# Sums of squares read one slot later, and scale products with one operand in PSUM, in a fused attention, SwiGLU and top-1 MoE kernel

## The chip, the core and the metric

The kernel runs on one core of a Trainium2 chip. The metric is device time in microseconds (us) of one execution. A measurement of this kernel is the median of several runs.

The core's engines run side by side, each through its own queue of instructions in order: TensorE (PE, with its weight loads shown as PEld), VectorE (DVE), ScalarE (ACT), GpSimd (POOL) and SyncE (SP), which here only issues DMAs. SBUF is the core's large memory, PSUM the small one into which TensorE writes.

## The reference

Three stages in a row; what one gives is the next one's input.

```python
# 1: attention with decay, B, H, S, D = 4, 8, 576, 64
scores = (q @ k^T) / sqrt(D)
cum = cumsum(log(clip(f, 0.0001, 1.0)))            # along the sequence
scores = where(causal, -1e9, scores + cum[:, :, :, None] - cum[:, :, None, :])
attn = softmax(scores);  x = (attn @ v)            # -> 2304 tokens x 512
# 2: SwiGLU, 512 -> 1536 -> 512
g = x @ w_gate;  y = (g * sigmoid(g) * (x @ w_val)) @ w_out
# 3: top-1 of 8 experts, 512 -> 1024 -> 512
e = argmax(y @ r_gate);  out = softmax prob of e * (relu(y @ w1[e]) @ w2[e])
```

## The kernel before, in words

Products are made from two 16-bit (or rounded 32-bit) halves of each operand. So that an operand fits 16 bits, it is first multiplied by a power of two that follows from its sum of squares. Such a scale is made in two steps. ACT squares the data and adds each partition's squares up (`accum_out`, into a tile `am` for q and k, `sq` for v, `totw` for the weights). Then `pow2_scale` asks TensorE for a tiny product with a matrix of eights (`onesf`), which leaves the total in each partition of a PSUM tile `tot`; three integer operations of DVE on one or two numbers turn it into a power of two, and a copy takes its inverse out. `tot` comes from the same ring of three PSUM banks (`ps_s`, tag `s`) as the score tiles `ps`.

The attention works on 16 pairs of heads (4 batches with 4 pairs). A pair has 4 items, and `slot(i)` records for item i: `part1(i)` (scores on TensorE, running maximum on DVE at L311, exponentials on ACT at L321), `part2(i - 1)` (16-bit halves of the probabilities: DVE's cast at L343, POOL's differences at L346 and L357, then a transposing DMA `pt<-p` at L360), `pv(i - 2)` (attention times v on TensorE, L381, and the normalised `xn`), and a piece of the next pair's preparation. For pair P + 1 that is `scales` with the first slot of pair P, `prep_v` with the second, `prep` for one head with the third and for the other with the fourth. `scales` holds the two squares (L189, their result `jk` is thrown away), `pow2_scale`, three tiny products `c` on DVE (L197) and a small ACT operation `nc` (L202). `prep` makes the halves `qks` of q and k on ACT (L224, L229) and DVE (L228) and issues the transposing DMA `qkt<-qks` (L231), without which the pair's scores can't begin (L256).

Beside the attention the SwiGLU weights are decoded and split, as a list of tasks: `w_dec` (a load, ACT, DVE, POOL, then squares on ACT at L866) for two halves of `w_gate`, `w_split` of it (`pow2_scale`, then ACT at L880 and DVE at L881), the same for `w_val`, and so on for six blocks. `unit(u)` is one block of SwiGLU on TensorE: `g` and `v` (L491), then `yp` (L544). Units run beside the later attention slots and go on alone after them; then come the experts (L1177, L1220).

What is recorded here is not the order in which the engines run it. The kernel is built with a scheduler (`schedule_with_timeline_sim=True`) that plays the program through with times of its own and writes each engine's queue from that. Semaphores and ring buffers follow that order.

Of the kernel before, what the change touches and what calls it, by code (L numbers as in the profile page):

```python
# [7 lines left out]
F32 = mybir.dt.float32  # L8
# [3 lines left out]
I32 = mybir.dt.int32  # L12
# [3 lines left out]
ALU = mybir.AluOpType  # L16
# [11 lines left out]
def kernel(  # L28
# [145 lines left out]
    def load_qk(P, a):  # L174
        if P < NPAIR:
            load_heads(qk_in[(2 * P + a) % NQK], (q, k)[a], P // NP, 2 * (P % NP))
# [5 lines left out]

    stt = {}

    def scales(P):
        am = st_p.tile([128, 2], F32, tag="am", bufs=2, name="am")
        jk = qks_p.tile([128, 3 * NCH, 2, D], F16, tag="qks", name="jk").rearrange("p (a c) h d -> p a c h d", a=3)
        for a in range(2):
            act.activation(  # L189
                out=jk[:, a].rearrange("p c h d -> p h c d"), in_=qk_in[(2 * P + a) % NQK], func=ACTF.Square,  # L190
                accum_out=am[:, a:a + 1],
            )
        sc = st_p.tile([128, 2, 2], F32, tag="sc", name="sc")
        pow2_scale(sc[:, 0, :], sc[:, 1, :], [am])
        c = st_p.tile([128, 3], F32, tag="c", name="c")
        for i, (w, f_) in enumerate(((1, 0.125), (0, 8.0), (1, -0.125))):
            vec.scalar_tensor_tensor(  # L197
                out=c[:, i:i + 1], in0=sc[:, w, 0:1], scalar=f_, in1=sc[:, w, 1:2], op0=ALU.mult, op1=ALU.mult
            )
        nc_ = st_p.tile([128, 2, 128], BF16, tag="nc", bufs=2, name="nc")  # L200
        h0 = P // NP * H + 2 * (P % NP)
        act.activation(  # L202
            out=nc_, in_=pick[:, h0:h0 + 2].rearrange("p (h o) -> p h o", o=1).to_broadcast([128, 2, 128]),
            func=ACTF.Copy, scale=c[:, 1:2],
        )
        stt[P] = (sc, (c, nc_))
# [29 lines left out]
    def prep_v(P):  # L236
        i = P % NV
        sb_ = sv[:, 0, P // NP:P // NP + 1]
        vs = vs_p.tile([128, 2, NCH, 2, D], F16, tag="vs", name="vs")
        for hh in range(2):  # L240
            src = v_in[i][:, hh]
            act.activation(out=vs[:, hh, :, 0, :], in_=src, func=ACTF.Copy, scale=sb_)
            vec.scalar_tensor_tensor(
                out=vs[:, hh, :, 1, :], in0=src, scalar=sb_, in1=vs[:, hh, :, 0, :], op0=ALU.mult, op1=ALU.subtract
            )
        vsp[P] = vs
# [193 lines left out]
    def slot(i):  # L440
        P = i // 4
        r = i % 4
        if i < NI:
            part1(i)
        if 0 <= i - 1 < NI:
            part2(i - 1)
        if 0 <= i - 2 < NI:
            pv(i - 2)
        if i % (4 * NP) == 10 and P // NP + 1 < B:
            v_scale(P // NP + 1)  # L450
        if P + 1 < NPAIR:
            if r == 0:
                scales(P + 1)
            if r == 1:
                prep_v(P + 1)
                if P + 2 < NPAIR:
                    load_v(P + 2)
            if r == 2:
                prep(P + 1, 0)
            if r == 3:  # L460
                prep(P + 1, 1)
                load_qk(P + 2, 1)
                load_qk(P + 3, 0)
# [305 lines left out]
        act.dma_start(out=y_d[NT:NT + 1, :], in_=zr)  # L769
        act.dma_start(out=g_d[NT:NT + 1, :], in_=zr[:, 0:1])  # L770

    def pow2_scale(dst, inv, parts):
        n = dst.shape[1]
        tot = ps_s.tile([128, 512], F32, tag="s", name="tot")[:, 0:n]
        for i, x in enumerate(parts):
            pe.matmul(
                out=tot, lhsT=onesf, rhs=x, start=(i == 0), stop=(i == len(parts) - 1), skip_group_check=True
            )
        ti = tot.bitcast(I32)
        vec.tensor_scalar(  # L780
            out=ti, in0=ti, scalar1=24, scalar2=23, op0=ALU.logical_shift_right, op1=ALU.logical_shift_left
        )
        vec.tensor_scalar(
            out=ti, in0=ti, scalar1=float(49 * EXP1), scalar2=float(48 * EXP1), op0=ALU.max, op1=ALU.add
        )
        vec.tensor_scalar(
            out=dst.bitcast(I32), in0=ti, scalar1=-1.0, scalar2=float(254 * EXP1), op0=ALU.mult, op1=ALU.add
        )
        vec.tensor_copy(out=inv, in_=tot)

    VB = H * S * D // 128
    vflat = v.rearrange("b h s d -> b (h s d)").rearrange("b (p n) -> b p n", p=128)
# [2 lines left out]
    def v_scale(b):  # L795
        sq = st_p.tile([128, 4], F32, tag="sq", bufs=1, name="sq")
        n = VB // 4
        for i in range(4):
            t = s_p.tile([128, 576], F32, tag="s", name="vr")[:, 0:n]
            sp.dma_start(out=t, in_=vflat[b, :, i * n:(i + 1) * n])  # L800
            act.activation(out=t, in_=t, func=ACTF.Square, accum_out=sq[:, i:i + 1])
        pow2_scale(sv[:, 0, b:b + 1], sv[:, 1, b:b + 1], [sq[:, i:i + 1] for i in range(4)])

    def unscale(b, j0, j1):
        rv = sv[:, 1, b:b + 1]
# [55 lines left out]
    def w_dec(j, i, h):  # L861
        f0 = 256 * j + 128 * h
        if h == 0:
            tops[j, i] = st_p.tile([128, 2], F32, tag="totw", name="totw")
        t = dec[j, i, h] = decode((w_gate, w_val)[i].rearrange("(k p) f -> p k f", p=128)[:, :, f0:f0 + 128], KD)
        act.activation(  # L866
            out=(wg16, wv16)[i][:, j, :, 0, 128 * h:128 * h + 128], in_=t, func=ACTF.Square,
            accum_out=tops[j, i][:, h:h + 1],
        )

    def w_split(j, i):
        tot = tops.pop((j, i))
        w16 = (wg16, wv16)[i]
        s1 = sw[:, 0, i, j:j + 1]
        pow2_scale(s1, sw[:, 1, i, j:j + 1], [tot[:, h:h + 1] for h in range(2)])
        for h in range(2):
            f0 = 128 * h
            src = dec.pop((j, i, h))
            hi, lo = w16[:, j, :, 0, f0:f0 + 128], w16[:, j, :, 1, f0:f0 + 128]
            act.activation(out=hi, in_=src, func=ACTF.Copy, scale=s1)  # L880
            vec.scalar_tensor_tensor(out=lo, in0=src, scalar=s1, in1=hi, op0=ALU.mult, op1=ALU.subtract)  # L881
# [11 lines left out]
    NJ = KF // 2  # L893
    tasks, mark, markw = [], {}, {}
    for j in range(NJ):
        for i in range(2):
            tasks += [lambda j=j, i=i, h=h: w_dec(j, i, h) for h in range(2)]
            tasks.append(lambda j=j, i=i: w_split(j, i))
        tasks.append(lambda j=j: unscale(0, j, j + 1))
        mark[j] = len(tasks)  # L900
        tasks += [lambda fk=fk: wo_dec(fk) for fk in (2 * j, 2 * j + 1)]
        markw[j] = len(tasks)
        if j >= NJ - 3:
            tasks.append(lambda j=j: free.__setitem__(0, [0, 1, 2] if j == NJ - 3 else [0]))
    done = [0]

    def upto(n):
        while done[0] < min(n, len(tasks)):
            tasks[done[0]]()
            done[0] += 1  # L910
# [195 lines left out]
    PRE0, PRE = 2, 43  # L1106
    start()
    upto(PRE0)
    scales(0)
    v_scale(0)  # L1110
    prep(0, 0)
    prep(0, 1)
    load_qk(1, 1)
    load_qk(2, 0)
    prep_v(0)
    load_v(1)
    first = 4 * NP + 2
# [321 lines left out]
```

## Time and profile before

| | |
|---|---|
| median of 3 runs | 1042.72 us (1039.12 to 1043.49) |
| the profiled execution's own time | 1036.55 us |
| its span, first to last instruction | 1034.8 us |
| busy share of the span | PE 86%, DVE 61%, ACT 54%, POOL 38% |
| mean granted TensorE clock | 0.933 |

The profiled execution is one run; its span lies 1.75 us below its own time and its time 6.2 us below the median of the three runs. Busy shares are means over stages that differ: the first 205 us hold the first attention slots and all the weight decoding, the stretch from 205 to 590 us the attention and SwiGLU together, and the rest SwiGLU alone, the routing and the experts.

### The profile page before, as it was taken

To read this page: it belongs to the slowest core of one execution; us is meant where nothing else is said; L and a number is where in the kernel's file an instruction comes from. 1 tells how busy PE (TensorE), PEld (TensorE's weight loads), DVE (VectorE), ACT (ScalarE), POOL (GpSimd) and SP (SyncE) were. 2 spreads that over 40 slices of the span, in tenths; PEclk is the share of its full clock that TensorE was granted. 3 is DMA by queue.
4 is the path that set the end of the run, shared out by engine and by line. 5 is a ranking of instruction groups with operands and counts; after the bars stand their busy time and mean duration, and the time that the engine had idled before them with its cause. 6 is when DMAs were issued, how large, how long until landed. Compare 5 with 4: busy or idle time off the path is not lost.

```text
span 1034.8 us, 19815 instructions
## 1 busy us (share of the span) xinstructions
PE 885.4 (86%) x7003; PEld 738.0 (71%) x7029; DVE 632.2 (61%) x1829; ACT 558.0 (54%) x1208; POOL 397.6 (38%) x473
## 2 busy tenths in 40 slices
PE   1545557989889988899899999999789899999995
PEld 0333436867667776788688878888668799899894
DVE  6999879497577575567765443234326787656440
ACT  5987988476576565556554231213225455555441
POOL 1567767364255234344444222222225643111101
PEclk9995557999999998999999999999898899999998
DMA  8897997258776768566754440203329987754430
GB/s 241 201 225 209 227 193 167 85 131 156 139 154 142 168 113 161 115 110 150 105 109 108 113 123 2 41 2 83 51 35 219 273 239 214 207 170 152 149 104 33
DMA packets 314409, 145.30 MB, mean 140 GB/s; under 512 B 279649, under 2 KB 292065, under 8 KB 314308
## 3 DMA queue, kind: packets, MB, share of 16 engines
q1 hardware_dynamic: 310016, 133.63, 55.7%
q0 software_dynamic: 4096, 10.24, 3.9%
q8 instruction: 56, 0.92, 0.4%
q14 instruction: 45, 0.37, 0.2%
q10 hardware_dynamic: 196, 0.14, 0.1%
HBM read 81.62 MB, written 10.31 MB: 89 GB/s over the span
## 4 chain that ended last, share of the span: by engine, by line
PE 42%; DMA 7%; issue 6%; ACT 3%; DVE 2%; POOL 2%; SPq 1%; POOLq 0%; DVEq 0%; ACTq 0%
PE bank L1220 9%; PE bank L1177 8%; PE yp L544 8%; PE v L491 7%; PE g L491 6%; DMA pair<-yt 1%; DMA out_dram<-o,ix 1%; POOL xg L1051 1%; PE px L381 1%; DMA qkt<-qks 1%; DMA pt<-p 1%; DMA pair<-words 1%; ACT st L321 1%; DMA wr<-in_moe_w_dram 1%; DVE st L311 1%
## 5 line engine op out<-in xcount | busy, mean ns | idle before, releaser
L491 PE MATMUL v<-xr,wv 128*128 128x256 f16 x1296 | 162.4, 281 | 0.0
L491 PE MATMUL g<-xr,wg 128*128 128x256 f16 x1296 | 161.4, 278 | 0.5 <-DMA xr<-xs 0.5
L491 PEld LDWEIGHTS <-wg 128*128 128x128 f16 x1296 | 123.6, 100 | 26.8 <-issue 9.2
L491 PEld LDWEIGHTS <-wv 128*128 128x128 f16 x1296 | 128.9, 101 | 18.9 <-issue 1.0
L346 POOL TENSOR_TENSOR p<-st,p 128x128 f16<-128x128 f32 (+3 forms) x128 | 108.7, 854 | 79.1 <-issue 52.4
L531 POOL TENSOR_TENSOR lo<-t,hi 128x512 fp32r<-128x512 f32 x54 | 71.5, 1324 | 148.6 <-ACT hi L530 123.4
L321 ACT ACTIVATE st<-st,nb,c 128x64 f32<-128x64 f32 (+4 forms) x160 | 102.6, 643 | 1.2
L381 PE MATMUL px<-vs,pt 128*128 128x64 f16 x1280 | 58.7, 203 | 41.0 <-DMA pt<-p 30.0
L343 DVE CAST p<-st 128x64 f16<-128x64 f32 (+4 forms) x160 | 71.8, 464 | 30.7 <-ACT st L321 21.9
L381 PEld LDWEIGHTS <-pt 128*128 128x128 f16 x1280 | 52.4, 106 | 52.4 <-DMA pt<-p 35.1
L514 ACT ACTIVATE t<-g,gscale 128x512 f32<-128x512 f32 (+3 forms) x72 | 39.3, 571 | 75.5 <-PE g L491 75.5
L256 PE MATMUL ps<-qkt 128*128 128x64 f16 (+2 forms) x192 | 56.7, 311 | 25.9 <-DMA qkt<-qks 11.3
L357 POOL TENSOR_TENSOR p<-st,p 128x64 f16<-128x64 f32 (+1 forms) x128 | 54.2, 425 | 61.5 <-DVE p L343 30.6
L1220 PE MATMUL bank<-whi,h 128*128 128x512 f32 x200 | 66.9, 400 | 4.8 <-ACT h L1182 4.8
L983 POOL DMA_INDIRECT out_dram<-o,ix x24 | 26.6, 1110 | 113.8 <-ACT o L1222 71.2
L311 DVE CUSTOM_DVE_ANT_0 st<-ps,zero 128x64 f32<-128x64 f32 (+3 forms) x160 | 55.6, 376 | 24.2 <-PE ps L264 21.0
L517 DVE SCALAR_TENSOR_TENSOR t<-t,g 128x512 f32<-128x512 f32 x54 | 36.9, 684 | 54.3 <-ACT t L514 54.2
L530 ACT ACTIVATE hi<-t 128x512 fp32r<-128x512 f32 x54 | 33.8, 625 | 60.8 <-DVE t L524 60.8
L949 DVE TENSOR_TENSOR wlo<-wr,whi 128x1024 fp32r<-128x1024 f32 x48 | 57.7, 1245 | 14.1 <-ACT whi L948 12.3
L257 PE MATMUL ps<-qkt 128*128 128x64 f16 (+2 forms) x192 | 59.9, 315 | 0.0
L544 PE MATMUL yp<-wohi,hi 128*128 128x512 f32 x144 | 59.7, 414 | 0.0
L1177 PE MATMUL bank<-xh,whi 128*128 128x320 f32 (+1 forms) x192 | 58.9, 309 | 0.5 <-ACT xh L93 0.5
(300 smaller groups left out, 2274.2 us busy)
## 6 DMA issues: line engine op xcount, KB each, us to landing
wr<-in_moe_w_dram SPq DMA_DIRECT2D x72, 512.0 KB
vr<-in_v_dram SPq DMA_DIRECT2D x16, 288.0 KB
qk_in<-in_q_dram SPq DMA_DIRECT2D x32, 128.0 KB
qk_in<-in_k_dram SPq DMA_DIRECT2D x32, 128.0 KB
v_in<-in_v_dram SPq DMA_DIRECT2D x32, 128.0 KB
y_d<-ys SPq DMA_DIRECT2D x6, 512.0 KB
wg<-in_moe_w_gate_dram SPq DMA_DIRECT2D x5, 512.0 KB
raw<-in_moe_w_val_dram SPq DMA_DIRECT2D x5, 512.0 KB
```

What stands on the lines that cost most here:

```text
L257: pe.matmul(out=ps[:, o:o + n], lhsT=lq, rhs=qkt[:, 2, k0:k1], start=False, stop=False, skip_group_check=True)
L311: vec.tensor_tensor_reduce(out=sts[m][:, k0 - 64:k1 - 64], in0=ps[:, o:o + n], in1=zero.to_broadcast([128, n]), scale=1.0, scalar=init, op ...
L321: act.activation(out=sts[m], in_=sts[m], func=ACTF.Exp, scale=c[:, 0:1], bias=nb[:, m:m + 1], accum_out=sm[:, m, hh:hh + 1],)
L343: vec.tensor_copy(out=flat[:, o + 64:o + 64 + n], in_=src)
L346: gp.tensor_tensor(out=flat[:, o1:o1 + n - 64], in0=src[:, 64:n], in1=flat[:, o + 128:o + 64 + n], op=ALU.subtract)
L381: pe.matmul(out=px[:, 128 * m + 64 * hh:128 * m + 64 * hh + 64], lhsT=pm[:, o + ph * last + c, :], rhs=vs[:, hh, c, vh, :], start=(c == 0 ...
L491: pe.matmul(out=ps[:, fi, :], lhsT=w16[:, j, kk, wi, 128 * fi:128 * fi + 128], rhs=xr[:, kk, x0:x0 + 2, xi, :], start=(n_ == 0), stop=(n_ ...
L531: last["lo"] = gp.tensor_tensor(out=lo, in0=t, in1=hi.bitcast(F32), op=ALU.subtract)
L544: pe.matmul(out=yps[g][i], lhsT=hx[:, fi, 128 * i:128 * i + 128], rhs=wo[fk][wx], start=(j == 0 and n_ == 0), stop=(j == KF // 2 - 1 and n ...
L949: (eng or vec).tensor_tensor(out=l_, in0=t, in1=h_.bitcast(F32), op=ALU.subtract)
L1177: pe.matmul(out=p, lhsT=w[wi][:, kk, 128 * fk:128 * fk + 128], rhs=x[xi][:, kk, c0:CAP], start=(n_ == 0), stop=(n_ == 3 * KD - 1),)
L1220: pe.matmul(out=p[0:m, :], lhsT=hx, rhs=wx, start=(n_ == 0), stop=(n_ == len(prods) - 1))
```

## The change

The squares become a function of their own, which stays with the first slot of a pair, and `scales`, with what reads the sums, moves to the second slot, ahead of `prep_v`. `pow2_scale` gets a tile with two rows: its total goes to the second column (or columns) of the PSUM tile, the power of two is written to the first ones in PSUM instead of SBUF, and one copy takes both to SBUF. The three products `c` read one operand from that PSUM tile and the other from the SBUF copy. In the list of weight tasks the split of `w_gate` moves behind the first half of `w_val`. At the start `v_scale(0)` moves behind the first pair's `prep`.

```diff
+    sqs = {}
+
+    def squares(P):
+        am = sqs[P] = st_p.tile([128, 2], F32, tag="am", bufs=2, name="am")
         jk = qks_p.tile(...)
         for a in range(2):
             act.activation(... func=ACTF.Square, accum_out=am[:, a:a + 1])
+
+    def scales(P):
         sc = st_p.tile([128, 2, 2], F32, tag="sc", name="sc")
-        pow2_scale(sc[:, 0, :], sc[:, 1, :], [am])
+        r = pow2_scale(sc, [sqs.pop(P)])
         ...
             vec.scalar_tensor_tensor(
-                out=c[:, i:i + 1], in0=sc[:, w, 0:1], scalar=f_, in1=sc[:, w, 1:2], op0=ALU.mult, op1=ALU.mult
+                out=c[:, i:i + 1], in0=r[:, w, 0:1], scalar=f_, in1=sc[:, w, 1:2], op0=ALU.mult, op1=ALU.mult
             )
...
             if r == 0:
+                squares(P + 1)
+            if r == 1:
                 scales(P + 1)
-            if r == 1:
                 prep_v(P + 1)
...
-    def pow2_scale(dst, inv, parts):
-        n = dst.shape[1]
-        tot = ps_s.tile([128, 512], F32, tag="s", name="tot")[:, 0:n]
+    def pow2_scale(both, parts):
+        n = both.shape[2]
+        ps = ps_s.tile([128, 512], F32, tag="s", name="tot")
+        tot = ps[:, n:2 * n]
...
-            out=dst.bitcast(I32), in0=ti, scalar1=-1.0, ...
+            out=ps[:, 0:n].bitcast(I32), in0=ti, scalar1=-1.0, ...
         )
-        vec.tensor_copy(out=inv, in_=tot)
+        r = ps[:, 0:2 * n].rearrange("p (w n) -> p w n", w=2)
+        vec.tensor_copy(out=both, in_=r)
+        return r
...
-        for i in range(2):
-            tasks += [lambda j=j, i=i, h=h: w_dec(j, i, h) for h in range(2)]
-            tasks.append(lambda j=j, i=i: w_split(j, i))
+        parts_ = [lambda j=j, i=i, h=h: w_dec(j, i, h) for i in range(2) for h in range(2)]
+        parts_.insert(3, lambda j=j: w_split(j, 0))
+        tasks += parts_
+        tasks.append(lambda j=j: w_split(j, 1))
...
+    squares(0)
     scales(0)
-    v_scale(0)
     prep(0, 0)
...
+    v_scale(0)
     prep_v(0)
```

No instruction is added or removed on PE, ACT or POOL, and on DVE none either: there the power of two goes to `tot` instead of `sc`, `sw` or `sv`, and the copy is twice as wide. What changes is the scheduler's order. PE's queue differs from its 28th row on, and its last 3,992 rows of 11,378 (from within the last pair's slots on) are the same again. Line numbers shift: L256 of before is L260 of after, L776 is L782, L197 is L201, L321 is L325, L224 is L228, L880 is L888.

PE, the scores of the first pair's first slot and what follows them (`tot<-am` is the tiny product on the second pair's squares, `tot<-totw` that on the weights' squares). Before:

```order
L264 LDWEIGHTS negid
L264 MATMUL ps<-maskgt,negid 128x128
L776 MATMUL tot<-am,onesf 128x2
L776 MATMUL tot<-totw,onesf 128x1 x2
L256 LDWEIGHTS qkt
L256 MATMUL ps<-qkt 128x64
```

And now at the end of the first pair's second slot:

```order
L268 LDWEIGHTS negid
L268 MATMUL ps<-maskgt,negid 128x128
L782 MATMUL tot<-am,onesf 128x2
L782 MATMUL tot<-totw,onesf 128x1 x2
L260 LDWEIGHTS qkt
L260 MATMUL ps<-qkt 128x448
```

The product on the squares has moved behind one more slot of scores (12 matmuls), here and at each later pair.

ACT, in the first pair's slots: `qks` and `nc` are the second pair's preparation, `st` the first pair's exponentials, `wg`, `wv` and `wo` the weight tasks. Before, where the preparation ends and the first slot's exponentials begin:

```order
L224 ACTIVATE qks<-qk_in_98,sc 128x2x5x64
L202 ACTIVATE nc<-pick,c 128x256
L321 ACT_TABLE_LOAD
L321 ACTIVATE st,sm<-st,nb,c 128x64
L321 ACTIVATE st,sm<-st,nb,c 128x192
L321 ACTIVATE st,sm<-st,nb,c 128x320
L880 ACTIVATE wg_92<-c,sw 128x4x128 x2
```

Now, at the end of the second slot's exponentials (the first slot's stand ahead of them, and the split of the first `wg` ahead of those):

```order
L325 ACTIVATE st,sm<-st,nb,c 128x64
L325 ACTIVATE st,sm<-st,nb,c 128x192
L325 ACTIVATE st,sm<-st,nb,c 128x320
L857 ACTIVATE wo<-wg_92 128x512
L228 ACTIVATE qks<-qk_in_100,sc 128x5x64
L888 ACTIVATE wv_93<-c,sw 128x4x128 x2
L228 ACTIVATE qks<-qk_in_98,sc 128x2x5x64
```

The next pair's preparation has moved from ahead of the exponentials of a slot to behind those of two slots, and the first split of the weights ahead of all of them.

DVE, at the three products `c` of the third pair (`xr` and `sm` belong to the attention's output, `wg` to a weight split). Before:

```order
L786 TENSOR_SCALAR sc<-tot 128x2
L789 COPY sc<-tot 128x2
L197 SCALAR_TENSOR_TENSOR c<-sc 128x1
L435 TENSOR_TENSOR xr<-px,xr 128x64
L197 SCALAR_TENSOR_TENSOR c<-sc 128x1 x2
L311 ISA st,mx<-ps,zero 128x64
L311 ISA mx 128x1
```

Now:

```order
L792 TENSOR_SCALAR tot<-tot 128x2
L439 TENSOR_TENSOR xr<-px,xr 128x2x128
L796 COPY sc<-tot 128x4
L201 SCALAR_TENSOR_TENSOR c<-tot,sc 128x1 x3
L889 SCALAR_TENSOR_TENSOR wg_92<-wo,sw,wg_92 128x4x128
L315 ISA st,mx<-ps,zero 128x448
```

The products read `tot` and `sc` instead of `sc` alone, and behind them stands a weight split with its operands in SBUF, where the maximum over a PSUM tile stood.

## Rows read from the trace of the kernel before

**Rows 1.** The page's first lines: the span, and the busy time of each engine with its share and its number of instructions.

```profile
span 1034.8 us, 19815 instructions
PE 885.4 (86%) x7003; PEld 738.0 (71%) x7029; DVE 632.2 (61%) x1829; ACT 558.0 (54%) x1208; POOL 397.6 (38%) x473
```

**Rows 2.** Stretches of the span: start and end, length, busy us (and instructions) of PE, PEld, DVE, ACT and POOL, granted clock, DMA share, GB/s. The last row is SwiGLU alone, behind the attention.

```profile
27.00:110.00 83.00, 43.72 (x353) 31.43 (x357) 78.84 (x211) 73.45 (x183) 53.75 (x58) 0.80 0.88 216
110.00:205.00 95.00, 69.16 (x585) 54.53 (x587) 70.40 (x192) 71.20 (x169) 59.12 (x62) 0.74 0.72 166
205.00:590.00 385.00, 354.28 (x3465) 288.38 (x3483) 252.59 (x890) 226.18 (x572) 168.07 (x235) 0.97 0.65 132
...
600.00:730.00 130.00, 129.62 (x993) 108.75 (x994) 44.72 (x154) 31.79 (x54) 29.69 (x27) 1.00 0.20 43
```

**Rows 3.** What PE waited for from 27 to 110 us: who waits and for whom, us in total, times, the longest.

```profile
PE px L381 <- DMA pt<-p: 14.3, 4, 5.1
PE px L423 <- DVE xn L394: 9.7, 3, 4.3
...
PE ps L256 <- DMA qkt<-qks: 5.8, 2, 3.9
PE tot L776 <- ACT c L849: 1.7, 1, 1.7
...
PE tot L776 <- ACT qks L224: 1.3, 1, 1.3
PE tot L776 <- ACT jk L189: 1.1, 1, 1.1
```

**Rows 4.** The same from 110 to 205 us.

```profile
PE px L381 <- DMA pt<-p: 6.1, 4, 2.1
PE ps L256 <- DMA qkt<-qks: 3.7, 1, 3.7
PE ps L256 <- DVE sw L789: 3.3, 1, 3.3
...
PE tot L776 <- ACT wg L866: 2.6, 2, 1.6
PE tot L776 <- ACT wv L866: 1.5, 1, 1.5
```

**Rows 5.** The same from 205 to 590 us.

```profile
PE px L381 <- DMA pt<-p: 9.6, 10, 1.8
PE tot L776 <- ACT vr L801: 7.7, 3, 3.9
...
PE ps L256 <- DVE sc L789: 1.8, 1, 1.8
PE ps L256 <- DMA qkt<-qks: 1.7, 1, 1.7
PE tot L776 <- ACT jk L189: 0.6, 1, 0.6
```

**Rows 6.** The products `c` of L197 alone: all 48 (duration in ns, least, median, most), then their busy time on DVE in three stretches, then three of them at one pair in the order of time (start, length).

```profile
L197 DVE SCALAR_TENSOR_TENSOR c<-sc x48: 145/154/1318, 10.3 to 516.9; 128x1 f32<-128x1 f32 x48
...
27.00:110.00 83.00, 4.40 (x9) 0.80 0.88 216
110.00:205.00 95.00, 1.16 (x6) 0.74 0.72 166
205.00:590.00 385.00, 7.38 (x30) 0.97 0.65 132
...
409.53 0.30 DVE L197 SCALAR_TENSOR_TENSOR c<-sc 128x1 f32<-128x1 f32 x3
```

**Rows 7.** DVE and POOL in the order of time at the third pair's products: start us, length us, engine, line, operation, tiles and shapes.

```profile
60.76 1.15 POOL L346 TENSOR_TENSOR p<-st,p 128x512 f16<-128x512 f32 x1
60.79 1.13 DVE L197 SCALAR_TENSOR_TENSOR c<-sc 128x1 f32<-128x1 f32 x1
...
61.98 1.45 DVE L197 SCALAR_TENSOR_TENSOR c<-sc 128x1 f32<-128x1 f32 x2
62.13 1.28 POOL L855 TENSOR_TENSOR wo<-wo,wv 128x512 f32<-128x512 f32 x1
63.35 0.21 DVE L311 CUSTOM_DVE_ANT_0 st<-ps,zero 128x64 f32<-128x64 f32 x1
```

**Rows 8.** The copy out of PSUM that ends `pow2_scale`, all 16 for q and k, in the groups by line up to 600 us: count, then busy us and mean ns, then the idle time before them.

```profile
L789 DVE COPY sc<-tot 128x2 f32<-128x2 f32 x16 | 2.4, 149 | 0.0
```

**Rows 9.** A cast of part2 beside a POOL operation, in the order of time.

```profile
91.81 1.15 POOL L346 TENSOR_TENSOR p<-st,p 128x512 f16<-128x512 f32 x1
91.88 1.14 DVE L343 CAST p<-st 128x64 f16<-128x64 f32 x1
```

**Rows 10.** From the product on the squares of the tenth pair to its first scores, in the order of time; in brackets the idle time before and what ended it. The score matmul at 309.62 us opens the ninth pair's third slot.

```profile
306.19 0.28 PE L776 MATMUL tot<-am,onesf 128*128 128x2 f32 x2
...
308.35 2.35 DVE L197 SCALAR_TENSOR_TENSOR c<-sc 128x1 f32<-128x1 f32 x3
309.62 0.35 PE L256 MATMUL ps<-qkt 128*128 128x448 f16 x1
...
314.48 1.52 SPq L231 DMA_TRANSPOSE qkt<-qks  x1
318.10 0.20 PE L256 MATMUL ps<-qkt 128*128 128x64 f16 x1 [1.70 <-DMA qkt<-qks]
```

More of the change, by code (lines that the diff above doesn't have):

```diff
@@ L183 @@
     stt = {}
-    def scales(P):
-        am = st_p.tile([128, 2], F32, tag="am", bufs=2, name="am")
+    sqs = {}
+    def squares(P):
+        am = sqs[P] = st_p.tile([128, 2], F32, tag="am", bufs=2, name="am")
         jk = qks_p.tile([128, 3 * NCH, 2, D], F16, tag="qks", name="jk").rearrange("p (a c) h d -> p a c h d", a=3)
@@ L786, in pow2_scale @@
         vec.tensor_scalar(
-            out=dst.bitcast(I32), in0=ti, scalar1=-1.0, scalar2=float(254 * EXP1), op0=ALU.mult, op1=ALU.add
+            out=ps[:, 0:n].bitcast(I32), in0=ti, scalar1=-1.0, scalar2=float(254 * EXP1), op0=ALU.mult, op1=ALU.add
         )
-        vec.tensor_copy(out=inv, in_=tot)
+        r = ps[:, 0:2 * n].rearrange("p (w n) -> p w n", w=2)
+        vec.tensor_copy(out=both, in_=r)
+        return r
     VB = H * S * D // 128
@@ L801, in v_scale @@
             act.activation(out=t, in_=t, func=ACTF.Square, accum_out=sq[:, i:i + 1])
-        pow2_scale(sv[:, 0, b:b + 1], sv[:, 1, b:b + 1], [sq[:, i:i + 1] for i in range(4)])
+        pow2_scale(sv[:, :, b:b + 1], [sq[:, i:i + 1] for i in range(4)])
     def unscale(b, j0, j1):
@@ L874, in w_split @@
         s1 = sw[:, 0, i, j:j + 1]
-        pow2_scale(s1, sw[:, 1, i, j:j + 1], [tot[:, h:h + 1] for h in range(2)])
+        pow2_scale(sw[:, :, i, j:j + 1], [tot[:, h:h + 1] for h in range(2)])
         for h in range(2):
```

## The prediction

> **What bounds the kernel now.** I read the page's first lines, then the stretches, then who waited for whom in each of them. The page says that PE is busy 885.4 of 1034.8 us, DVE 632.2 [rows 1]. That is a mean over stages that differ, so the reader should look at the stretches [rows 2]. From 600 to 730 us PE works 129.62 of 130.00 us: there and later it is the bound, the queues are the same in both programs, and what is won or lost ahead of it moves the end by as much. From 205 to 590 us PE is busy 354.28 of 385.00 us (92%) and DVE 252.59 (66%): PE bounds it, and what counts is PE's remaining 31 us of waits. From 27 to 110 us it is the other way round: DVE is busy 78.84 of 83.00 us (95%), ACT 73.45, PE only 43.72. There a wait of PE costs nothing, and a microsecond of DVE costs about one. From 110 to 205 us PE (69.16 of 95.00), DVE (70.40) and ACT (71.20) are all near three quarters: nothing alone bounds it, chains do. The granted clock there is 0.74, in the 83 us before it 0.80; both stretches are ones in which PE waits a lot, so I read no cost of its own from that.
>
> What PE waits for is mostly not what the change touches. From 27 to 110 us the transposed probabilities cost it 14.3 us and the normalised `xn` 9.7, the tiny products 1.7 + 1.3 + 1.1 us [rows 3]. From 110 to 205 us the tiny products wait 2.6 + 1.5 us for the weights' squares [rows 4]. From 205 to 590 us they wait 7.7 us for the squares of v and 0.6 us for those of q and k [rows 5].
>
> **The change, part by part.** It adds and removes no instruction; each part moves work or changes an operand.
>
> The three products of a pair take 0.30 us together when nothing disturbs them, as at 409.53 us [rows 6]. Their median is 154 ns, but the longest takes 1318 ns. The reader sees why in the order of time [rows 7]: the product that starts at 60.79 us ends at 61.92, POOL's operation that began at 60.76 ends at 61.91; two more take 1.45 us from 61.98 and end at 63.43, POOL's from 62.13 ends at 63.41. A product with two SBUF operands waits out a POOL operation. With one operand in PSUM I expect none to. [...]
>
> From 27 to 110 us the nine products take 4.40 us [rows 6]; undisturbed it would be 3 x 0.30 = 0.90, so 3.5 us can go, on the engine that bounds the stretch. The lower end is nothing, because the wait may pass to the next operation: the order now puts a weight split with SBUF operands behind the third pair's products, where a maximum over PSUM stood, and a cast from SBUF waits for POOL just as well (1.14 us for 64 columns beside POOL's 1.15 [rows 9]). I take half, 1.8 us. From 110 to 205 us it is 1.16 - 0.60 = 0.6 us and from 205 to 590 us 7.38 - 3.00 = 4.4 us, on an engine with a quarter to a third of its time free; bounds 0 and 5.0 us, and I take 0, because only 1.8 us of PE's waits there are for the copy just ahead of these products [rows 5]. If DVE's free time were not there, the 4.4 us would count.
>
> Against that stands what the PSUM operand costs. The nearest row is the copy out of the same tile, 149 ns [rows 8], against the products' median of 154 ns from SBUF [rows 6]: no difference, so 0. [...]
>
> The squares a slot ahead: PE no longer stands behind ACT's squares. That wait is 0.6 us from 205 to 590 us [rows 5], which counts in full, and 1.1 us in the DVE-bound stretch [rows 3], which counts nothing. Lower end 0, I take 0.6.
>
> The split of `w_gate` behind a further decode gives its squares more time: the 2.6 us for `wg` from 110 to 205 us can go, the 1.5 us for `wv` stay, since that split still follows its own squares [rows 4]. PE is not alone the bound there, so between 0 and 2.6 I take half, 1.3 us. `v_scale(0)` behind the first `prep` I cost at 0: the scheduler's queues begin with the same rows in both programs, on PE through the first slot's scores.
>
> The PSUM tile is now held until the products are through instead of the copy, 0.30 us more, in a ring of three banks that the scores share. What is queued behind it on PE are those scores; today they wait 1.8 us for that copy in 205 to 590 us [rows 5]. Lower end 0, upper end 0.30 at each of 16 pairs, 4.8 us; I take 0.6, two such waits.
>
> The scales a slot later leave less time for `prep`. The cover is one or two slots of scores and SwiGLU on PE; where that is gone the scores wait for `qkt`, which they do now for 5.8 + 3.7 + 1.7 us [rows 3 to 5]. I take no growth; the price is with the rivals.
>
> Sum: -1.8 - 0.6 - 1.3 + 0.6 = -3.1 us. Against the profiled execution's 1036.55 us (span 1034.8 [rows 1] and 1.75 around it) that is 1033.4. The median of the runs shown, 1042.72, lies 6.2 us above that execution; by the median I forecast 1042.7 - 3.1 = 1039.6 us. The terms' ends alone reach from -3.5 - 5.0 - 0.6 - 2.6 = -11.7 to +4.8 us, 1031 to 1047.5.
>
> **The rivals.**
> *Larger gain.* The scheduler rewrites the queues up to the last pair's slots, and the new order may fill what idles now. In 110 to 205 us DVE has 24.6 us free and PE 25.8 [rows 2]; a third of that, 8 us, with the 3.1 gives 1031.6. For it: the waits on the tiny products are spread out in the new queues and the weights' tasks are closer together. Against it: the largest waits of PE, on `pt` (14.3, 6.1, 9.6 us [rows 3 to 5]), hang on DVE, POOL and DMA, which have the same work.
>
> *No gain at all.* The port's wait passes on to the casts, the splits' wait was hidden, and the change does not do what it says; PE's waits on the squares were only 1.7 us to begin with [rows 3, 5]. 1042 to 1043 us.
>
> *Slower.* The scores of the next pair wait for `qkt`, because `prep` starts a slot late. At the tenth pair [rows 10] the product is asked for at 306.19 us, three slots ahead of its scores, the products end at 310.70, the transposing DMA is issued at 314.48, and the scores at 318.10 have still waited 1.70 us. With a slot less ahead of it that chain of 11.9 us has only two slots to hide behind. If 8 of the 15 later preparations are as tight and wait once more as long, it costs 8 x 1.70 = 13.6 us, less the 3.1: 1053. It decides from 5 such waits on (8.3 us, which with the gain is 5.2 over). Against it: from 27 to 590 us the scores waited for `qkt` only four times [rows 3 to 5], and the scheduler had the later place before it when it laid out the SwiGLU work around it.
>
> **How the numbers follow.** A measurement of this kernel can tell about 0.5%, 5.2 us, from no change. The forecast (a gain of 0 to 5 us) has 0.36, no gain (0 to 5 us slower included) 0.10, the larger gain 0.34, slower 0.20. Of the forecast 0.02 falls beyond 5.2 us, so faster has 0.34 + 0.02 = 0.36, within 0.5% has 0.34 + 0.10 = 0.44, and slower 0.20. The predicted time is 1039.6. Its own range is 1036 to 1043; the range for 8 in 10 takes in most of the larger gain, down to 1029, and the slower case to the terms' end and a little of the late `qkt`, 1048.
>
> **What would show it.** In the changed profile: the 48 products between 140 and 200 ns each, none near 1.3 us, and some casts or splits behind them longer instead; PE's tiny products on `am` without a wait for `jk`; fewer waits for `wg`, those for `wv` as before; PE's waits for `qkt` still near 11 us. From 27 to 110 us the same work should be through about 2 us sooner. It would be wrong if the scores wait for `qkt` at most pairs, if the products still stretch beside POOL, or if the stretch to 205 us moves by more than 5 us for reasons of order alone.

## The result, and the profile after

The changed kernel takes 1053.81 us (median of 5, 1052.25 to 1058.22) against 1042.72 us; the ratio is 1.0118, 95% interval 1.0090 to 1.0145. The ratios here and below are the recorded estimates over all runs of both kernels; they differ from the quotients of the medians, here 1.0106, by up to 0.2%. It is slower, and outside the predicted range. Its profiled execution took 1058.22 us, 4.4 above its median, that of before 1036.55, 6.2 below: the two traces lie 21.7 us apart, the medians 11.1. So I read from the traces where time is lost and take the size from the medians.

The page's first lines of the changed kernel, then its stretches (columns as in [rows 2]):

```profile
span 1056.4 us, 19859 instructions
PE 888.7 (84%) x7029; PEld 737.3 (70%) x7029; DVE 626.0 (59%) x1829; ACT 558.4 (53%) x1208; POOL 392.3 (37%) x473
```

```profile
27.00:110.00 83.00, 45.75 (x356) 32.44 (x357) 74.54 (x215) 74.93 (x186) 51.00 (x61) 0.81 0.89 215
110.00:205.00 95.00, 60.81 (x492) 46.92 (x492) 66.27 (x175) 67.29 (x160) 53.85 (x56) 0.70 0.67 160
205.00:590.00 385.00, 348.25 (x3440) 281.57 (x3439) 248.58 (x891) 225.56 (x572) 166.15 (x230) 0.97 0.67 127
600.00:730.00 130.00, 128.68 (x998) 108.00 (x997) 44.63 (x131) 33.00 (x56) 30.36 (x26) 1.00 0.23 59
```

Against [rows 1, 2]: DVE is busy 6.2 us less over the span, and PE has the same work. From 27 to 110 us PE is even busy 2.0 us more; from 110 to 205 us it is busy 8.4 us less, from 205 to 590 us 6.0 us less. The loss lies in the attention; SwiGLU alone (600 to 730 us) is as full as before to 1 us. The granted clock from 205 to 590 us is 0.97 of full speed in both traces, so the loss there is waiting and not a slower clock.

PE's waits of the changed kernel, from 27 to 110 us, from 110 to 205 us and from 205 to 590 us (who waits and for whom, us in total, times, the longest):

```profile
PE ps L260 <- DMA qkt<-qks: 12.8, 3, 6.0
PE px L385 <- DMA pt<-p: 9.7, 5, 2.8
...
PE tot L782 <- ACT wg L874: 0.6, 1, 0.6
...
PE px L385 <- DMA pt<-p: 8.9, 3, 7.8
PE ps L260 <- DVE xn L398: 5.5, 1, 5.5
...
PE tot L782 <- ACT wv L874: 2.9, 1, 2.9
...
PE ps L260 <- DMA qkt<-qks: 1.6, 1, 1.6
...
PE ps L260 <- DMA qkt<-qks: 19.4, 7, 6.4
PE px L385 <- DMA pt<-p: 9.6, 8, 3.1
...
PE tot L782 <- ACT vr L809: 1.6, 1, 1.6
```

The wait of the scores for `qkt` was 5.8 + 3.7 + 1.7 = 11.2 us in 4 waits [rows 3 to 5]; it is 12.8 + 1.6 + 19.4 = 33.8 us in 11. The waits of the tiny products for `jk` are gone. The rows of `qkt`, first of the kernel before, then of the changed one: the first matmul of each score group (count; least, median, most ns; first and last start in us), the transposing DMA's issue on SP, and the idle time ahead of these rows that `qkt` ended (us, times). The last figure adds PE's matmuls and PE's weight loads, so most waits stand in it twice; PE's own share is 11.3 us before and 33.8 now.

```profile
L256 PE MATMUL ps<-qkt x192: 189/299/634, 27.0 to 571.5; 128*128 128x64 f16 x64, 128*128 128x192 f16 x32, 128*128 128x320 f16 x32, 128*128 128x448 f16 x32
L231 SPq DMA_TRANSPOSE qkt<-qks x32: 1511/1659/4360, 21.2 to 536.7; - x32
  DMA qkt<-qks: 26.0, 10
```

```profile
L260 PE MATMUL ps<-qkt x192: 192/300/616, 27.5 to 586.8; 128*128 128x64 f16 x64, 128*128 128x192 f16 x32, 128*128 128x320 f16 x32, 128*128 128x448 f16 x32
L235 SPq DMA_TRANSPOSE qkt<-qks x32: 1347/1658/6853, 21.7 to 550.3; - x32
  DMA qkt<-qks: 76.4, 23
```

The last scores start at 586.8 instead of 571.5 us, 15.3 us later. At the tenth pair, which [rows 10] shows of before, the changed trace reads in the order of time:

```profile
325.15 0.34 PE L782 MATMUL tot<-am,onesf 128*128 128x2 f32 x2
...
327.79 0.16 DVE L201 SCALAR_TENSOR_TENSOR c<-tot,sc 128x1 f32<-128x1 f32 x1
329.01 0.21 DVE L201 SCALAR_TENSOR_TENSOR c<-tot,sc 128x1 f32<-128x1 f32 x2
...
338.33 1.53 SPq L235 DMA_TRANSPOSE qkt<-qks  x1
342.25 0.20 PE L260 MATMUL ps<-qkt 128*128 128x64 f16 x1 [1.29 <-DMA qkt<-qks]
```

The three products take 0.16 + 0.21 us instead of 2.35 [rows 10], and the last of them ends 4.1 us after the tiny product's start instead of 4.5, but the preparation behind them takes longer: from the last of them to the issue of the transposing DMA it is 9.1 us against 3.8, and from the tiny product to the scores 17.1 us against 11.9. The longest of the waits lies at another pair, where the transposing DMA is issued behind another transpose and a load:

```profile
282.18 1.19 SPq L421 DMA_TRANSPOSE xr<-xs  x1
283.43 0.58 SPq L170 DMA_DIRECT2D qk_in<-in_k_dram  x1
284.10 6.85 SPq L235 DMA_TRANSPOSE qkt<-qks  x1
...
294.56 0.24 PE L260 MATMUL ps<-qkt 128*128 128x64 f16 x1 [6.42 <-DMA qkt<-qks]
```

After another transpose (`xr`) and a load its issue holds SP 6.85 us instead of the median 1.66, and the scores come 10.5 us after it; at the tenth pair it is 3.9 us.

### The profile page after: what moved, and what is told of

Same layout as the page of the kernel before. It is cut to its first block, busy times and chain, and to the rows that moved or that the text cites. A ratio compares the mean times of both kernels' runs of the same rounds, so it can differ in the third digit from the quotient of the medians.

```text
span 1056.4 us, 19859 instructions
## 1 busy us (share of the span) xinstructions
PE 888.7 (84%) x7029; PEld 737.3 (70%) x7029; DVE 626.0 (59%) x1829; ACT 558.4 (53%) x1208; POOL 392.3 (37%) x473
## 5 line engine op out<-in xcount | busy, mean ns | idle before, releaser
L496 PE MATMUL v<-xr,wv 128*128 128x256 f16 x1296 | 159.9, 276 | 1.0 <-DVE wv L889 0.6
L496 PEld LDWEIGHTS <-wv 128*128 128x128 f16 x1296 | 126.2, 100 | 19.8 <-issue 2.3
L325 ACT ACTIVATE st<-st,nb,c 128x64 f32<-128x64 f32 (+4 forms) x160 | 102.8, 645 | 1.9
L260 PE MATMUL ps<-qkt 128*128 128x64 f16 (+2 forms) x192 | 57.0, 314 | 51.8 <-DMA qkt<-qks 33.8
L992 POOL DMA_INDIRECT out_dram<-o,ix x24 | 24.4, 1015 | 110.9 <-ACT o L1232 71.5
L535 ACT ACTIVATE hi<-t 128x512 fp32r<-128x512 f32 x54 | 33.8, 625 | 59.9 <-DVE t L529 59.9
L260 PEld LDWEIGHTS <-qkt 128*128 128x128 f16 x192 | 22.3, 116 | 58.1 <-DMA qkt<-qks 42.6
L321 ACT ACTIVATE nb<-mx,addc,c 128x3 f32<-128x3 f32 (+1 forms) x64 | 24.5, 383 | 68.3 <-DVE mx L315 67.5
```

The costliest lines, as they stand in the source:

```text
L260: pe.matmul(out=ps[:, o:o + n], lhsT=lq, rhs=qkt[:, 1, k0:k1], start=True, stop=False, skip_group_check=True)
L325: act.activation(out=sts[m], in_=sts[m], func=ACTF.Exp, scale=c[:, 0:1], bias=nb[:, m:m + 1], accum_out=sm[:, m, hh:hh + 1],)
L496: pe.matmul(out=ps[:, fi, :], lhsT=w16[:, j, kk, wi, 128 * fi:128 * fi + 128], rhs=xr[:, kk, x0:x0 + 2, xi, :], start=(n_ == 0), stop=(n_ ...
```

## The experiments

Four theories stand in the expectations. **Theory 1**: the later scales make `prep` late, and the scores wait for `qkt`. **Theory 2**: the weight order does it. **Theory 3**: the PSUM tile, held longer, keeps the scores out. **Theory 4**: the scheduler's new order of the queues costs by itself, whatever the edit. Below, W is the weight order, P the PSUM operand with the two-row `pow2_scale`, S the split of squares and scales, each as in the change's diff. Moving `v_scale(0)` leaves every engine's queue as it was. All ratios are to the kernel before on the same chip, whose median there was 1028.9 to 1042.7 us; where an expectation names microseconds, they are counted from 1042.7. Each kernel has one trace.

### Each part alone

S alone, its hunks of the change and nothing else:

```diff
             if r == 0:
-                scales(P + 1)
+                squares(P + 1)
             if r == 1:
+                scales(P + 1)
```

> The kernel before with the one edit that the scales are read a slot after the squares; products and weight order as before. Theory 1 (the scores of the next pair wait for qkt because prep starts a slot late): 1049 to 1058 us, and PE's waits for qkt from 27 to 590 us above 25 us (before 11.2, changed kernel 33.8). Theory 2 (the new order of the weight splits starts SwiGLU late): 1040 to 1045, waits for qkt near 11. Theory 3 (the PSUM tile is held until the products are through): 1040 to 1045.

Measured: 1048.45 us, 1.0084 (1.0054 to 1.0114). PE's waits from 27 to 610 us:

```profile
PE ps L260 <- DMA qkt<-qks: 41.3, 13, 9.8
PE px L385 <- DMA pt<-p: 31.0, 22, 3.6
```

So S alone costs, within theory 1's range by the ratio, and the wait that theory 1 names has grown with it from 11.3 us.

W and P without S:

> The changed kernel with the scales back in the squares' slot: PSUM operand and new weight order stay. Theory 1: 1032 to 1043, waits for qkt under 15 us. Theory 2: 1049 to 1056, the second unit's first g at 175 us or later (before 168.6, changed kernel 177.8). Theory 3: 1046 to 1056.

Measured: 1048.58 us, 1.0093 (1.0053 to 1.0133). The waits for `qkt` are near those of before, and others have grown:

```profile
PE px L381 <- DMA pt<-p: 37.5, 20, 5.2
PE px L381 <- DVE xr L435: 17.5, 5, 6.0
PE ps L256 <- DMA qkt<-qks: 14.7, 6, 4.2
PE tot L777 <- ACT jk L189: 8.0, 4, 6.3
```

A second loss of the same size, then, in which the late scales have no part. Theory 2's sign came: the second unit's `g` starts at 176.0 us. Theory 3's did not: the scores wait 1.5 us in all for the products `c`. W alone:

> The kernel before with the one edit that the split of w_gate stands behind the first half of w_val. Theory 1: 1036 to 1043, PE's wait for wg squares from 110 to 205 us (2.6) gone. Theory 2: 1048 to 1055 and the second unit's g at 175 us or later. Theory 3: 1040 to 1045.

Measured: 1040.74 us, 1.0015 (0.9987 to 1.0042). But the wait for `wg` from 110 to 205 us is still there (2.7 us). P alone:

> The kernel before with the one edit that the power of two stays in PSUM and the products read one operand there. Theories 1 and 2: 1036 to 1043, each product 140 to 200 ns. Theory 3: 1047 to 1056, PE waiting for the banks (scores that wait for the products or their copy) 5 us or more over the 2.3 of before.

Measured: 1037.17 us, 0.9993 (0.9969 to 1.0018). Here the scores wait 0.3 us for `c`, and the second unit's `g` starts at 174.6 us without a loss. Neither part costs alone in this order of the queues, and the 0.93% of the two together stays unexplained. In none of the eight traces with P do the scores wait more than 1.5 us for the products `c` or the copy `sc`, so theory 3 falls by its own sign.

### How late the scales are

S alone, with the scales at the head of the second slot, ahead of its scores (half the delay). The edit moves more than the expectation says: the next pair's `prep_v` and its load stand a slot earlier too, with the squares.

```diff
         r = i % 4
+        if r == 1 and P + 1 < NPAIR:
+            scales(P + 1)
         if i < NI:
...
             if r == 0:
-                scales(P + 1)
-            if r == 1:
+                squares(P + 1)
                 prep_v(P + 1)
```

> The kernel before with the scales read at the head of the second slot, ahead of that slot's scores, instead of behind them: half the delay of the run squares_alone (1.0084 of before, PE's waits for qkt 41.3 us). Theory 1 (lateness of prep sets the loss): waits for qkt between 11 and 41 us, and a ratio between 1.000 and 1.008. Theory 4 (any rewriting of the queues costs something, whatever its sense): a ratio without relation to the waits for qkt, 1.003 to 1.012 with waits near 11 too.

Measured: 1047.18 us, 1.0059 (1.0029 to 1.0089); waits for `qkt` 22.6 us. S alone, with the scales in the third slot, ahead of `prep`:

```diff
             if r == 1:
-                scales(P + 1)
                 prep_v(P + 1)
...
             if r == 2:
+                scales(P + 1)
                 prep(P + 1, 0)
```

> The kernel before with the squares in the first slot and the scales in the third, just ahead of prep: twice the delay of squares_alone. Theory 1: PE's waits for qkt 50 us or more, ratio 1.012 to 1.025. Theory 4: ratio 1.003 to 1.012, like the others.

Measured: 1071.04 us, 1.0296 (1.0249 to 1.0342). PE's waits from 27 to 610 us:

```profile
PE ps L260 <- DMA qkt<-qks: 36.3, 11, 9.5
PE px L385 <- DMA pt<-p: 35.0, 21, 4.8
PE px L385 <- DVE xr L439: 21.9, 6, 7.1
PE px L427 <- DVE xn L398: 16.0, 5, 5.3
PE g L496 <- ACT xr L438: 10.0, 3, 4.6
```

By delay (none, half a slot, one, two) the ratio is 1.0000, 1.0059, 1.0084, 1.0296. That rises with the lateness, but half a slot and one lie within each other's intervals, and the half has `prep_v` moved besides; only two slots stand out. The wait expected for it does not follow: 36.3 us for `qkt` is less than with half this delay. The rest shows as waits for `pt`, `xr` and `xn` (30.0, 3.1 and 10.4 us before), so the loss need not show at the wait that the late preparation names.

The whole change with the scales half as late (the first hunk above alone, `prep_v` where it was):

> The whole change, but the scales (with what reads the sums) recorded at the head of the second slot, ahead of its scores, instead of behind them: half the delay. Theory 1 by its dose (1.0059 against 1.0084 when the late scales were alone) expects 0.25% below the changed kernel, 1.009 or less, with waits for qkt of about 23 us instead of 33.8. If only the order that the other two parts bring counts, it stays at 1.009 to 1.012 whatever the waits for qkt do.

Measured: 1049.60 us, 1.0072 (1.0049 to 1.0095), waits for `qkt` 12.4 us. Less delay, less loss, as theory 1 says, though the two intervals (the change's begins at 1.0090) still touch; and back at the `qkt` waits of before it is still slower than before.

### The parts in the whole change

All of it, the products from SBUF alone:

```diff
-                out=c[:, i:i + 1], in0=r[:, w, 0:1], scalar=f_, in1=sc[:, w, 1:2], ...
+                out=c[:, i:i + 1], in0=sc[:, w, 0:1], scalar=f_, in1=sc[:, w, 1:2], ...
```

> The changed kernel with one edit: the three products read both operands from the SBUF copy again. The queues stay almost the same (56 of some 11,400 rows of PE differ, 8 of DVE), so this prices the PSUM operand by itself. If the wait for POOL that it removes is worth something on the path: 2 to 4 us above the changed kernel (1.014 to 1.016 of before), with products that take up to 1.3 us again. If that wait only passes on or is hidden: within 1.5 us of the changed kernel (1.0105 to 1.0135).

Measured: 1056.83 us, 1.0139 (1.0095 to 1.0183). The order of the queues hardly differs, so this is the operand by itself. The 48 products of the changed kernel, then of this one (least, median, most ns):

```profile
L201 DVE SCALAR_TENSOR_TENSOR c<-tot,sc x48: 142/148/159, 10.4 to 537.1; 128x1 f32<-128x1 f32 x48
```

```profile
L201 DVE SCALAR_TENSOR_TENSOR c<-sc x48: 145/154/901, 10.4 to 539.8; 128x1 f32<-128x1 f32 x48
```

The operand in PSUM does take the long products away: the longest is 159 ns against 901. In time it is worth some 2 us (1.0139 against 1.0118), less than these runs can tell from nothing; the measured ratio falls between the two expected ranges. P and S without W:

> The changed kernel with the old order of the weight splits. Theory 1: 1.008 to 1.014 of before, waits for qkt above 25 us, since the late scales stay. Theory 2 (weight order with the PSUM operand makes the loss, as all_but_squares 1.0093 suggests): 1.000 to 1.005.

Measured: 1057.95 us, 1.0152 (1.0113 to 1.0191), waits for `qkt` 38.6 us. Theory 2's 1.000 to 1.005 is far off: the weight order is not the loss. W and S without P:

> The weight order and the late scales, the products with both operands in SBUF. Theory 1 (late scales are the loss, the weight order nothing): 1.0084 + 0.0015, 1.008 to 1.011. Theory 4 (each rewritten order has a price of its own, up to half a per cent): anywhere from 1.004 to 1.014. That the PSUM operand is what adds up in pairs is borne out if this stays at or below 1.010, the two pairs with it being 1.0093 to 1.0152.

Measured: 1045.59 us, 1.0162 (1.0128 to 1.0195), waits for `qkt` 34.6 us: above every expectation. The parts don't add, and a single order of the queues may carry a price of its own.

### Another order of the same work

The halves of each decoded weight block are taken in the other order. They have the same shapes, and the total that both splits need has both, so no mechanism of the change is in this edit; but the scheduler writes other queues.

```diff
-        if h == 0:
+        if (j, i) not in tops:
...
-            tasks += [lambda j=j, i=i, h=h: w_dec(j, i, h) for h in range(2)]
+            tasks += [lambda j=j, i=i, h=h: w_dec(j, i, h) for h in (1, 0)]
```

The kernel before with it:

> The kernel before with the two halves of each decoded weight block taken in the other order (h = 1, then 0). The halves have the same shapes and the same work, and what reads them needs both, so no mechanism of the change is in it; only the scheduler writes other queues (on PE some 7,000 lines of difference). Theory 1 (the late preparation of q and k is the loss) expects 1.000 within 0.003 and PE's waits for qkt near the 11.3 us of before. Theory 4 (a rewritten order by itself moves the time by about one per cent either way) expects a ratio that may lie anywhere from 0.99 to 1.01; it is borne out if it is outside 0.997 to 1.003.

Measured: 1046.49 us, 1.0042 (1.0013 to 1.0072), and 25.2 us of waits for `qkt` with nothing late by design: theory 4's sign, if a small one. W and P with it:

> The weight order and the PSUM operand without the late scales (1.0093 as it was), with the halves of each decoded block exchanged as well. If those 0.93% come from something that the two parts do together, they stay: 1.007 to 1.012. If they are an accident of that one order of the queues (theory 4), another order of the same work gives another time: nearer 1.000, below 1.006.

Measured: 1054.52 us, 1.0121 (1.0098 to 1.0144): the loss stays in this order too. The whole change with it:

> The whole change with the halves of each decoded block exchanged. Theory 1: the late preparation is in it as before, so it stays slow, 1.008 or more, with waits for qkt of 25 us or more. Theory 4: it may lie anywhere within a per cent of the 1.0118, and below 1.004 would say that the late scales were no cause of their own.

Measured: 1052.56 us, 1.0113 (1.0085 to 1.0142): slow as theory 1 says, but with 21.5 us for `qkt`, less than its 25. S alone, P alone and W alone with it:

> The late scales alone, with the halves of each decoded block exchanged. Theory 1: the price of the late scales is there in this order too: 0.4% or more above the kernel before with exchanged halves (1.0042), so 1.008 or more. Theory 4 alone (no price of their own): as likely below 1.0084 as above it, around 1.004, and 1.005 or less bears it out.

Measured: 1045.21 us, 1.0167 (1.0131 to 1.0202): the price is there, and greater than in the first order.

> The PSUM operand alone, halves exchanged. If it is free, it stays at the 1.0042 of the exchanged halves, 1.001 to 1.007. If 0.9993 was a lucky order, or if it costs as soon as the weights come in another order (as it does with the new weight order, 1.0093), it gives 1.008 or more.

Measured: 1042.23 us, 1.0143 (1.0105 to 1.0181), where P alone in the first order was 0.9993. PE's waits from 205 to 590 us begin with:

```profile
PE px L381 <- DMA pt<-p: 12.4, 12, 2.0
PE tot L777 <- ACT jk L189: 6.2, 2, 5.8
```

> The weight order alone, halves exchanged. If it is free: 1.001 to 1.007, as the exchanged halves alone. If 1.0015 was a lucky order: 1.008 or more.

Measured: 1030.49 us, 1.0005 (0.9979 to 1.0031). And the last two of the eight combinations, W with S and P with S:

> The weight order and the late scales, the halves of each decoded block exchanged. If the late scales cost in every order: 1.008 or more, as the five kernels with them did. If their price is an accident of the order: as likely as not below 1.006.

Measured: 1051.98 us, 1.0105 (1.0074 to 1.0136).

> The PSUM operand and the late scales, the halves exchanged. If the late scales cost in every order: 1.008 or more. As the PSUM operand alone with exchanged halves is already at 1.0143, a price that adds would give up to 1.024; one that doesn't add, 1.012 to 1.017.

Measured: 1062.21 us, 1.0203 (1.0173 to 1.0233).

### The sixteen together

The last two columns are read from 205 to 565 us, which ends before the last scores start in any trace: PE's waits for `qkt`, and all of PE's idle time (360 us less its busy time). Where a column has two figures, the second is with exchanged halves.

| parts | first order | halves exchanged | PE's waits for `qkt`, 27 to 610 us | last scores start, us | `qkt`, 205 to 565 us | PE idle, 205 to 565 us |
|---|---|---|---|---|---|---|
| none | 1.0000 | 1.0042 | 11.3, 25.2 | 571.5, 578.3 | 1.7, 9.4 | 30.6, 30.4 |
| W | 1.0015 | 1.0005 | 12.0, 14.0 | 575.0, 567.0 | 6.1, 1.7 | 31.4, 26.7 |
| P | 0.9993 | 1.0143 | 14.0, 13.1 | 572.1, 579.7 | 6.1, 1.8 | 25.9, 29.0 |
| W P | 1.0093 | 1.0121 | 14.7, 19.0 | 585.1, 588.7 | 3.7, 2.7 | 37.9, 32.7 |
| S | 1.0084 | 1.0167 | 41.3, 19.3 | 583.9, 582.3 | 21.0, 12.9 | 39.4, 39.2 |
| W S | 1.0162 | 1.0105 | 34.6, 26.5 | 585.0, 584.2 | 15.5, 19.4 | 37.6, 35.7 |
| P S | 1.0152 | 1.0203 | 38.6, 30.5 | 587.2, 589.0 | 19.3, 18.3 | 36.9, 40.2 |
| W P S (the change) | 1.0118 | 1.0113 | 33.8, 21.5 | 586.8, 581.5 | 19.4, 8.5 | 35.9, 36.2 |

The sixteen ran on several chips, and most pairs that are compared below did not share one. That a ratio carries over from chip to chip was not tested. On one chip stand only S against none (+0.84%), W P S against W P with exchanged halves (-0.08%), and the exchange against none (+0.42%); three of the four kernels measured on the chip with 1028.9 us are among the five slowest by ratio.

**S.** The mean of the eight with S is 1.0138, of the eight without 1.0052: 0.87%, or 9 us of 1042.7. Of the eight pairs that differ by S alone seven are slower with it; their spread gives an interval of 0.4 to 1.4%, if they are taken as independent. The last scores start 7.8 us later in the mean (585.0 against 577.2), so nearly all of it arises ahead of them.

Where it arises can be told from the traces. From 27 to 205 us, where PE is not the bound, S makes no difference to PE's idle time (69.3 us in the mean with it, 71.4 without). From 205 to 565 us it does: PE waits for `qkt` in all eight pairs longer with S, 16.8 against 4.2 us in the mean, and idles 37.6 against 30.6 us, longer in seven of eight. So of 12.6 us of new waits 7.1 are left; what S saves there are mostly waits of the tiny products for the squares, of v (3.4 us) and of q and k, `jk` (2.8 us). Over the whole attention the waits for `qkt` alone are a poor measure of the price: with exchanged halves S alone waits 5.9 us less for `qkt` than none, and is 1.25% slower.

S does not add the same everywhere. Where W and P are not both there it costs 0.60 to 1.59%; in the two pairs with both, the change's own surroundings, 0.25 and -0.08%, and PE's idle time there changes by -2.0 and +3.5 us only. S taken out of the change gives next to nothing back.

**P.** 1.0117 with, 1.0073 without: 0.45%, interval 0.0 to 0.9%, which includes no price at all. Six of eight pairs are slower. Without S it is 0.72% in the mean, with S 0.17%. With P and without S the waits for `jk` are 2.7, 8.0, 8.4 and 6.2 us, without both 1.8, 4.3, 1.9 and 0.8: PE comes to the product on the squares while ACT is still at them, and S is what takes that wait away. Whether that is P's price, or P has one, is not settled.

**W.** 1.0092 with, 1.0098 without: nothing in the mean. It hangs on the order: in the first one W costs 0.40% in the mean of four, with exchanged halves it gains 0.53%, in all four pairs.

**The order alone.** Exchanging the halves moves one kernel by -0.57% (W S) to +1.50% (P), each of the two measured on two chips. P's is borne out by its traces: PE idles 81.6 instead of 65.7 us from 27 to 205 us, and 29.0 instead of 25.9 us from there to 565. The one by -0.57% is not: PE idles 104 us in both from 27 to 565 us. Of the other six, none (+0.42%) and S (+0.83%) are clear of the error, P S (+0.51%) barely. An order can cost as much as any part of the change.

## Why the prediction was wrong

**The step that failed** is "The scales a slot later leave less time for `prep` ... I take no growth". The waits for `qkt` grew from 11.2 to 33.8 us in this trace; the step's term was 0, and S costs 9 us in the mean of eight pairs, net of what it saves, by waits for `qkt` in the stretch that PE bounds. The rival "Slower" had the mechanism; that 8 x 1.70 us also gave it the number, 1053, is luck. It got 0.20. The growth was 7 waits with 22.6 us, not 8 of 1.7, and the longest, 6.42 us, came where the issue of the transposing DMA held SP 6.85 us behind a transpose and a load. What I held against it misled me twice. Four waits in 563 us showed that the slack was used up at four places, not that there was more at the others: [rows 10] had a chain of 11.9 us that ended in a wait with three slots ahead of it. And that the scheduler laid out its queues with the later place before it was no protection.

**A second step failed with it**: the terms of W and P, -1.3 - 1.8 + 0.6 = -2.5 us in the sum. Together, without S, the two measured +0.93%, 9.7 us, and 0.79% over the exchanged halves alone. Each of the two losses, S and W P, is nearly as large as the whole, and they don't add: with W and P there, S costs 0.25 and -0.08%. So the late scales are a sufficient cause of a loss of this size, not the only one. Why W and P cost together is open, and so is why P alone does with exchanged halves (1.0143); the PSUM tile, held longer, is not the reason (1.5 us of waits at most).

**An order without a price.** I gave the rewriting of the queues a chance of a gain ("Larger gain", 0.34) and none of a loss, though the last of the signs of being wrong names it. The exchanged halves alone cost 0.42% and moved four of eight kernels up by 0.4% or more and one down by as much, and the kernel before is the second fastest of the eight without S: four of the other seven, three of them with P, are slower beyond their intervals, none is faster. How far such an effect goes into the 11.1 us of this change can't be told from one kernel. That the sum of the single parts (0.84 + 0.15 - 0.07 = 0.92%) comes near 1.18% is chance, since W and P without S make 0.93% by themselves.

**DVE as the bound to 110 us.** "A microsecond of DVE costs about one" is not borne out. The products fell to 142 to 159 ns, as forecast, and DVE's work in this stretch from 78.84 to 74.54 us; PE was busy 2.0 us more there, and that gain is not seen any more at 205 us. P alone, whose queues differ too, shows the same (columns as in [rows 2]):

```profile
27.00:110.00 83.00, 43.38 (x324) 29.87 (x322) 75.66 (x212) 76.18 (x187) 54.59 (x58) 0.63 0.89 216
```

DVE is 3.2 us less busy than before, with 212 instructions instead of 211, and PE's are 324 instead of 353: nothing came sooner. The time freed on DVE went into its idle time. P alone measured 0.9993, and with the operand alone taken back the change costs 2 us more, within the error, so the 1.8 us taken for it stays unproven.

**Right.** No product stretches beside POOL any more: the longest of the 48 takes 159 ns, before it was 1318 [rows 6]. That an operand in PSUM would do this was my expectation, for which the prediction had no row; the two traces show it, but not what makes a product wait. What the rival "No gain at all" calls the port's wait is the time beside POOL in [rows 7]; no run shows a port. The PSUM operand itself costs DVE no time that shows: a median of 148 ns against 154 with both operands in SBUF. The waits for `jk` went, as the squares' slot ahead should do; the forecast had 0.6 us for it, and it is 3.8 us in the mean of eight.

**Right by luck.** PE's wait for `wg` fell from 2.6 us to none from 110 to 205 us, while that for `wv` rose from 1.5 to 2.9. But with W alone the wait for `wg` is still 2.7 us, and with P alone it is gone: the weight order did not do it, and the 1.3 us taken for it have no run behind them.

## What to carry to other kernels

Where an asynchronous chain ends in a wait of a microsecond or two at some turns, its slack is zero there, and a later start can cost at the turns like it: price the move by the whole chain against the cover that is left, with the DMA in it. Beside the waits that grow, read the whole idle time of the engine that waits: here 12.6 us of new waits came to 7.1. Where a scheduler writes the queues, change something that brings no mechanism of its own, such as the order of two equal loads, and see how far the time moves; here that was 0.5% in the mean and 1.5% in one case. A part is judged by its mean over several such orders, and by what is lost without it in the company in which it will stand, not by one kernel with it.

## What the runs showed of the hardware

In the changed kernel's trace the issue of a transposing DMA (`qkt`) held SP's queue for 1.66 us in the median of 32 and for 6.85 us, the longest, behind another transpose and a load. The scores that waited for it came 10.5 us after this issue began, and 3.9 us after one of 1.53 us at the tenth pair.

The 48 products of DVE on 128x1 numbers with both operands in SBUF had a median of 154 ns and a longest time of 1318 ns in the kernel before, of 154 and 901 ns in the changed kernel with its products from SBUF; with one operand in PSUM the changed kernel's had a median of 148 ns, and none took longer than 159 ns.

The kernel before had a median of 1039.1 to 1042.7 us on most chips and of 1028.9 us on one, where P and S with exchanged halves stood at 1042.2 and 1045.2. These medians lie 1.0 to 1.3% apart, about as much as the change costs, so each ratio here is to the kernel before on the same chip.
